# A delta-rule recurrence and a gated MLP on one core: weight pieces 768 columns wide, a shared gate and value bank, and a new division of PSUM

## The chip, the core and the metric

The kernel runs on one core of one Trainium2 chip. Its engines are TensorE (PE in the profile, its weight loads PEld), VectorE (DVE), ScalarE (ACT), GpSimd (POOL) and SyncE (SP, whose queue issues most of the transfers). The metric is the device time of one execution in microseconds (us), the median of several runs. The result must agree with a float32 reference.

## The reference

Four batches of eight heads run a delta rule over 768 tokens with head size 48; the 32 sequences are then read as 3072 tokens of 384 features for a gated MLP.

```python
k_n = k / (np.linalg.norm(k, axis=-1, keepdims=True) + 1e-06)
for t in range(S):
    kt, vt, bt = (k_n[:, :, t], v[:, :, t], beta[:, :, t, None])
    y[:, :, t] = np.einsum('bhd,bhde->bhe', q[:, :, t], state)
    v_old = np.einsum('bhde,bhd->bhe', state, kt)
    state = state + bt[:, :, :, None] * np.einsum('bhd,bhe->bhde', kt, vt - v_old)
...
gate = 1.0 / (1.0 + np.exp(-(x @ w_gate)))
val = x @ w_val
return (gate * val @ w_out).astype(np.float32)
```

The three weight matrices (384 x 1536 twice, 1536 x 384) arrive as float64 and are turned into float32 on the chip.

## The kernel before

**Recurrence.** The 768 tokens are cut into 12 groups of 64 (`g` = 0 to 11). Inside a group the recurrence is a triangular system: `gram` makes the products of all keys of a group, ScalarE and VectorE copy them to a tile G (`block`) with tokens along the free axis, `norms` takes the keys' norms from its diagonal and makes `gam` (beta over the squared norm) and `mq` (the norm, by which V is multiplied in `scale_v`), and a solve on VectorE inverts the system with two instructions a step. Groups are solved in pairs. For groups 0 and 1, `solve_pair` takes halves of 16 tokens (15 steps), transposes the result into `mt` (L334), and TensorE joins the halves: `pz`, a copy of it on ScalarE, `pm`, and a subtraction on VectorE (`closing`, L343), with a transpose (`flipped`, L339) ahead of `pm`. Later pairs are solved in 31 steps (`solve`, L298 and L301) and transposed at L303. After that come, for each group, the products with the state (`pk`), their subtraction from V (`less`, L384), the new rows (`updates`, `pu`, in steps 0 to 2), the output rows (`rows`, `yy`, from keys and queries masked on VectorE, L271) and the state's advance (`pd`). `flip` transposes the output rows into the MLP's input, split into two fp32r parts, high and low.

**Weights.** A weight piece is 128 x 384. There are 36, each loaded by one transfer of 384 KB (`load_piece`), and five instructions make it ready: on ScalarE `tail_bits` (L150), `rescale` (L155) and `weight_hi` (L167), on VectorE `join` (L162) and `weight_lo` (L172).

**MLP.** A tile is one unit of tokens by one of the 12 slices of the hidden layer. Groups 0 and 1 are a unit of 256 columns each (`single` tiles, 24 in all); later pairs of groups share a unit of 512 columns (`wide` tiles, 60). Each tile has nine matmuls for the gate and nine for the value (`gate_val`, L503), a sigmoid on ScalarE (L508), a product on VectorE (L513), a split into two parts (L518 on ScalarE, L523 on VectorE) and nine matmuls into three output banks (`outp`, L538). At a unit's end ScalarE copies the banks into `ot` tiles (L550) and SP stores them (L556).

**PSUM and SBUF.** The eight PSUM banks are three for the recurrence (`ps_aux`), two for gates and values, three for outputs (which some steps of groups 0 and 1 borrow). The tiles `u` (a joined weight piece) and `ot` share one SBUF tag of three buffers.

**Order.** No loop sets the order. Every step above is a `task` with an engine, an estimated cost, the tasks it follows, and the banks or buffers it takes and frees; `schedule` simulates the engines with those estimates, picks on each engine the ready task with the highest urgency (path length, the table URGENCY, a lift for the recurrence's words), and the kernel is then written out in that order. So each engine runs a fixed sequence, and what the estimates miss shows as waiting. Where the simulated TensorE has nothing to do ahead of the first gate, dummy matmuls on zeros (`warm_up`) are written in. Transfers are held back: at most EARLY groups of them are in flight up to the task named in QUIET (`pm0`), FLIGHT behind it, and the weight pieces from number HUSH on wait for that task.

Of the kernel before, what the change touches and what calls it, by code (L numbers as in the profile page):

```python
# [58 lines left out]
def deltanet_gated_mlp(ctx: ExitStack, tc: tile.TileContext, kd, qd, kv, beta, words, out):  # L59
# [97 lines left out]
    us = {}  # L157

    def join(n):
        half, lo, hi = words_of(n)  # L160
# [1 line left out]
        nc.vector.scalar_tensor_tensor(out=u, in0=hi, scalar=3, in1=lo, op0=ALU.logical_shift_left, op1=ALU.bitwise_or)  # L162

    def weight_hi(n):
        f, w = pieces[n]
        parts[w, f] = t = wt.tile([128, 2, PW], F32R, name=f"w_{n}", tag=f"w{n}")
        nc.scalar.copy(t[:, 0], us[n].bitcast(F32))  # L167
# [57 lines left out]
    def scale_v(g):  # L225
        V, mq = state[g]["v"], state[g - g % 2]["mq"]
        if g < 2:
            nc.vector.tensor_tensor(out=V, in0=V, in1=mq[:, :, g:g + 1].to_broadcast([128, CP, D]), op=ALU.mult)
# [751 lines left out]
```

## Time and profile before

| | |
|---|---|
| median of 3 runs | 657.55 us (654.12 to 658.02) |
| the profiled execution | 657.68 us |
| its span from the first to the last instruction | 656.0 us |
| PE busy | 624.8 us, 95% |
| PEld busy (beside PE) | 505.6 us, 77% |
| DVE busy | 389.0 us, 59% |
| ACT busy | 299.1 us, 46% |
| POOL busy | 10.1 us, 2% |
| moved by DMA | 40.77 MB |

The rows quoted further down are of the profiled execution. A row of a group names the line, the engine, the operation, output <- input and the shapes; behind the bar stand busy time, mean ns of one, and the idle time of the engine just ahead of such instructions with what ended it. A row of a timeline gives the start in us, the length, the engine and the instruction, and in square brackets how long the engine had stood still and what ended that. Busy shares are means over the whole span: the span has a first stretch in which TensorE has little work, and then one of tiles, and their limits differ.

### The profile page before, as it was taken

What the parts mean: (1) busy time and instruction counts of PE and PEld (TensorE: products, weight loads), DVE (VectorE), ACT (ScalarE), POOL (GpSimd) and SP (SyncE); (2) the same over time, 40 slices, a digit from 0 to 9 for tenths busy, and PEclk for the clock granted to TensorE, in tenths of its full rate; (3) what the DMA queues carried; (4) which work ended last, traced back from release to release, by engine and by line L of the source; (5) the groups of instructions that cost most, each with busy time, mean ns of one, the idle gap of its engine ahead of it and who ended that gap; (6) DMA issues with size and microseconds to landing.
All of it is one profiled execution on the core that took longest, in us unless ns stands there. A gap on an engine that the chain in (4) does not pass through costs nothing.

```text
span 656.0 us, 21070 instructions
## 1 busy us (share of the span) xinstructions
PE 624.8 (95%) x9420; PEld 505.6 (77%) x9420; DVE 389.0 (59%) x891; ACT 299.1 (46%) x720; POOL 10.1 (2%) x25
## 2 busy tenths in 40 slices
PE   8977898988999999999999999999999999999997
PEld 4446788977988787887778777778887778888886
DVE  4987859984589752599543499633699433221221
ACT  5777896445441635434415532724535323221212
POOL 3000000000000000000000000000000000000000
PEclk9978989999899999999999999999999999999999
DMA  8866650013130030120131021041020000010001
GB/s 274 266 165 203 195 171 26 1 27 107 29 82 24 26 84 27 33 74 25 27 108 34 2 72 48 4 108 35 1 73 25 3 2 3 0 49 0 1 0 49
DMA packets 16075, 40.77 MB, mean 62 GB/s; under 512 B 2929, under 2 KB 3697, under 8 KB 15985
## 3 DMA queue, kind: packets, MB, share of 16 engines
q1 hardware_dynamic: 15984, 39.43, 20.3%
q8 instruction: 74, 1.21, 0.8%
q14 instruction: 17, 0.13, 0.1%
HBM read 34.70 MB, written 4.72 MB: 60 GB/s over the span
## 4 chain that ended last, share of the span: by engine, by line
PE 66%; DVE 16%; DMA 9%; ACT 5%; issue 3%; SPq 1%; DVEq 0%
PE gv_g L503 18%; PE gv_v L503 18%; PE po L538 18%; DMA raw<-in_words_dram 6%; DVE tmp L298 3%; DVE X L301 3%; PE pu L405 3%; PE yy L433 2%; PE yy L436 1%; DVE sg L513 1%; ACT G L251 1%; PE pp L266 1%; DVE h L523 1%; PE pt L485 1%; PE pk L375 1%
## 5 line engine op out<-in xcount | busy, mean ns | idle before, releaser
L538 PE MATMUL po<-h,w 128*128 128x512 f32 (+1 forms) x756 | 169.9, 368 | 3.2 <-DVE h L523 2.6
L503 PE MATMUL gv_v<-xx,w 128*128 128x512 f32 (+1 forms) x756 | 167.4, 365 | 2.9 <-DVE w L172 2.4
L503 PE MATMUL gv_g<-xx,w 128*128 128x512 f32 (+1 forms) x756 | 168.0, 367 | 0.1
L538 PEld LDWEIGHTS po<-h,w 128*128 128x128 f32 x756 | 128.2, 189 | 28.3 <-DVE h L523 3.5
L503 PEld LDWEIGHTS gv_v<-xx,w 128*128 128x128 f32 x756 | 127.7, 189 | 26.6 <-DVE w L172 2.6
L503 PEld LDWEIGHTS gv_g<-xx,w 128*128 128x128 f32 x756 | 127.3, 189 | 23.3 <-DVE w L172 0.3
L513 DVE TENSOR_TENSOR sg<-sg,gv_v 128x512 f32<-128x512 f32 (+1 forms) x84 | 51.2, 609 | 124.1 <-PE gv_v L503 112.7
L518 ACT CAST h<-sg 128x512 fp32r<-128x512 f32 (+1 forms) x84 | 46.9, 559 | 150.6 <-DVE sg L513 150.3
L508 ACT ACTIVATE sg<-gv_g 128x512 f32<-128x512 f32 (+1 forms) x84 | 45.0, 536 | 97.8 <-PE gv_g L503 97.1
L523 DVE TENSOR_TENSOR h<-sg,h 128x512 fp32r<-128x512 f32 (+1 forms) x84 | 51.4, 612 | 30.0 <-ACT h L518 29.5
L413 ACT COPY su<-pu 32x384 f32<-32x384 f32 x92 | 43.3, 470 | 45.6 <-PE pu L405 44.1
L298 DVE TENSOR_TENSOR tmp<-X,gp 128x31 f32<-128x31 f32 (+15 forms) x155 | 53.0, 342 | 4.4
L301 DVE TENSOR_TENSOR X<-X,tmp 128x31 f32<-128x31 f32 (+15 forms) x155 | 52.9, 341 | 3.8
L232 ACT ACTIVATE v<-v,mq 128x48 f32<-128x48 f32 x160 | 37.7, 322 | 8.9 <-DVE mq L222 8.9
L384 DVE TENSOR_TENSOR R<-v,pk 128x384 f32<-128x384 f32 x44 | 22.3, 548 | 24.9 <-PE pk L398 17.1
L271 DVE TENSOR_TENSOR kqp<-pp,pmask 64x512 f32<-64x512 f32 x48 | 32.4, 686 | 6.5 <-PE pp L266 5.9
L469 DVE TENSOR_TENSOR su<-su,pd 48x384 f32<-48x384 f32 x40 | 22.0, 551 | 17.0 <-PE pd L460 16.4
L251 ACT COPY G<-pg 32x256 f32<-32x256 f32 (+1 forms) x66 | 25.8, 392 | 12.2 <-PE pg L247 10.9
L181 PE MATMUL warm<-zero 128*128 128x512 bf16 x104 | 27.7, 418 | 1.0 <-POOL half L116 1.0
L494 DVE TENSOR_TENSOR xx<-pt,xx 128x384 fp32r<-128x384 f32 x24 | 12.8, 554 | 21.7 <-ACT xx L492 21.4
L405 PEld LDWEIGHTS pu<-R,mt 32*32 32x32 f32 x1408 | 16.9, 105 | 11.2 <-issue 7.7
L405 PE MATMUL pu<-R,mt 32*32 32x48 f32 x1408 | 20.1, 203 | 4.7 <-issue 2.5
(89 smaller groups left out, 459.3 us busy)
## 6 DMA issues: line engine op xcount, KB each, us to landing
raw<-in_words_dram SPq DMA_DIRECT2D x36, 384.0 KB, 4.0
kqp<-in_qd_dram SPq DMA_DIRECT2D x24, 256.0 KB, 3.9
kqp<-in_kd_dram SPq DMA_DIRECT2D x24, 192.0 KB, 3.5
v<-in_kv_dram SPq DMA_DIRECT2D x12, 384.0 KB, 4.0
k<-in_kv_dram SPq DMA_DIRECT2D x12, 384.0 KB, 3.2
out_dram<-ot SPq DMA_DIRECT2D x15, 256.0 KB, 2.0
out_dram<-ot SPq DMA_DIRECT2D x6, 128.0 KB, 2.7
beta<-in_beta_dram SPq DMA_DIRECT2D x6, 16.0 KB, 4.0
```

The source lines that it names most:

```text
L232: nc.scalar.activation(V[:, c], V[:, c], AF.Copy, scale=mq[:, c, g % 2:g % 2 + 1])
L271: nc.vector.tensor_tensor(out=kq[t:t + 64, sec], in0=pp[e][t:t + 64], in1=pmask[t:t + 64, e].unsqueeze(1).to_broadcast([64, J, C]), op=ALU ...
L298: nc.vector.tensor_tensor(out=tmp, in0=X[:, j:32, j:j + 1].to_broadcast([128, n, j]), in1=gp[:, j:j + 1, 0:j].to_broadcast([128, n, j]), o ...
L301: nc.vector.tensor_tensor(out=X[:, j:32, 0:j], in0=X[:, j:32, 0:j], in1=tmp, op=ALU.add)
L405: nc.tensor.matmul(out=pu[0 if g else x][r:r + 32, j], lhsT=mt[r:r + 32, g % 2, e * J + j], rhs=R[e][r:r + 32, j], start=True, stop=True)
L413: nc.scalar.copy(su[r:r + 32, 3 if x else e], pu[0][r:r + 32])
L503: nc.tensor.matmul(out=pg, lhsT=parts[w, f][:, a, k * 128:(k + 1) * 128], rhs=x[b][:, k], start=(k == 0 and q == 0), stop=(k == KC - 1 and ...
L508: nc.scalar.activation(h, st["g", f], AF.Sigmoid)
L513: nc.vector.tensor_tensor(out=h, in0=h, in1=st["v", f], op=ALU.mult)
L518: nc.scalar.copy(hh[:, 0], st["sg", f])
L523: nc.vector.tensor_tensor(out=hh[:, 1], in0=st["sg", f], in1=hh[:, 0].bitcast(F32), op=ALU.subtract)
L538: nc.tensor.matmul(out=po[k], lhsT=parts["o", f][:, w, k * 128:(k + 1) * 128], rhs=hh[:, a], start=begins(p, f) and q == 0, stop=ends(p, f ...
```

## The change

- **Weight pieces.** 18 pieces of 768 columns: gate and value of one slice of the hidden layer ("gv"), or the output weights of two slices ("oo"). Each comes in two transfers of 384 KB and is converted by the same five instructions, each over 768 columns. EARLY is 3 and HUSH 6 (pieces, so twelve transfers).
- **PSUM.** Four banks for the recurrence, two for gates and values, two for outputs. A single tile's gate and value share a bank, and so do two of its three output parts; the third output bank of a wide tile comes from `ps_aux`. The masked products of group 0 move to `ps_out`, its `pk` and `pu` to `ps_aux`.
- **`u` and `ot`** have two buffers instead of three.
- **Norms.** `gam` is made from s² + 2 EPS s + EPS² right behind the root; the steps for the norm m come after it, and the solve now waits for `gam` alone. One step more.
- **`scale_v`** is one VectorE instruction for every group; for groups 2 to 11 it was 16 small ones on ScalarE.
- **Transfers.** One of group 0's two key transfers is issued by ScalarE.
- **`rows`** leaves out the products with the state for group 0, which are zero.
- **Order.** A single tile's gate and value are one task; estimates, URGENCY and the lifts have new numbers.

```diff
-EARLY, FLIGHT, HUSH = 4, 2, 15
+EARLY, FLIGHT, HUSH = 3, 2, 6
...
-    ps_aux = ctx.enter_context(tc.tile_pool(name="ps_aux", bufs=3, space=PSUM))
+    ps_aux = ctx.enter_context(tc.tile_pool(name="ps_aux", bufs=4, space=PSUM))
...
-    ps_out = ctx.enter_context(tc.tile_pool(name="ps_out", bufs=3, space=PSUM))
+    ps_out = ctx.enter_context(tc.tile_pool(name="ps_out", bufs=2, space=PSUM))
...
+        if g == 0:
+            nc.scalar.dma_start(*pairs.pop())
+        move(pairs)
...
+    pieces = []
+    for f in range(0, NF, 2):
+        pieces += [(f, "gv"), (f + 1, "gv"), (f, "oo")]
...
+    def load_piece(n, part):
+        if part == 0:
+            raw[n] = wt.tile([128, 2 * PW, 2], U32, name=f"raw_{n}", tag=f"w{n}")
+        mine = slice(part * 2 * PW, (part + 1) * 2 * PW)
+        move([(raw[n].rearrange("p c w -> p (c w)")[:, mine], words[n, :, mine])])
...
-        us[n] = u = wk.tile([128, PW], U32, name=f"u_{n}", tag="u", bufs=3)
+        us[n] = u = wk.tile([128, 2 * PW], U32, name=f"u_{n}", tag="u", bufs=2)
...
+        nc.vector.scalar_tensor_tensor(out=m, in0=s, scalar=2 * EPS, in1=ss, op0=ALU.mult, op1=ALU.add)
+        yield
+        nc.vector.tensor_scalar(out=m, in0=m, scalar1=EPS * EPS, scalar2=None, op0=ALU.add)
+        yield
+        st["gam"] = gam = wk.tile([128, 32], F32, name=f"gam_{g}", tag="gam", bufs=2)
+        nc.vector.reciprocal(gam, m)
...
-        nc.vector.tensor_tensor(out=t, in0=m, in1=m, op=ALU.mult)
-        yield
-        st["gam"] = gam = wk.tile([128, 32], F32, name=f"gam_{g}", tag="gam", bufs=2)
-        nc.vector.reciprocal(gam, t)
...
-        if g < 2:
-            nc.vector.tensor_tensor(out=V, in0=V, in1=mq[:, :, g:g + 1].to_broadcast([128, CP, D]), op=ALU.mult)
-            yield
-            return
-        for c in range(CP):
-            nc.scalar.activation(V[:, c], V[:, c], AF.Copy, scale=mq[:, c, g % 2:g % 2 + 1])
-            yield
+        nc.vector.tensor_tensor(out=V, in0=V, in1=mq[:, :, g % 2:g % 2 + 1].to_broadcast([128, CP, D]), op=ALU.mult)
+        yield
...
-            for part in range(2):
+            for part in range(0 if g else 1, 2):
...
+        if w == "g" or p > 1:
+            whole = ps_gv.tile([128, 512], F32, name=f"gv_{p}_{f}_{w}", tag="gv")
+            st["g", f], st["v", f] = (whole[:, 0:GT], whole[:, GT:2 * GT]) if p < 2 else (whole if w == "g" else st["g", f], whole)
+        pg = st[w, f]
...
-        st["ot", k] = ot = wk.tile([128, st["width"]], F32, name=f"ot_{p}_{k}", tag="u", bufs=3)
+        st["ot", k] = ot = wk.tile([128, st["width"]], F32, name=f"ot_{p}_{k}", tag="u", bufs=2)
...
-    URGENCY = {"G2": 16500, "L2": -3500, "T0": 10500, "bits/15": 26000, "bits/18": 7000, "gate0": 500, "gate1": -500, "gram0": -10500, "hh0": -15500, "hl0": 11000,
...
+    URGENCY = {"D0": -6500, "G3": -1000, "bits/0": -2000, "bits/12": -8500, "bits/15": 18500, "dk2": -3000, "dv1": -4500, "gate1": 1000, "gram3": 1500, "hh1": 500,
...
-    HEAD, LIFT, CHAIN = 60000, 20000, set("gram pk pp u yy pd pt less s y xh xl T D z pz pm m sv G L".split())
+    LIFTS = {0: 60000, 1: 10000, 2: 0, 3: 0}
+    FIRST = set("gram u yy pt less y xh xl T D z pz pm sv G n h mt ll".split())
+    CHAIN = set("gram pk pp u yy pd pt less s y xh xl T D z pz pm m sv G L".split())
```

What follows shows three places on VectorE in the written order, before and after. A row is a line of the kernel, an operation, output<-input with the tiles' numbered names, and the shape; x2 is two alike in a row.

VectorE before, from the second Newton step of group 0's norms (`ny`, `nt`, `ns`, `m`) to the start of its solve (`stage` holds the solution, `gp` the products of keys). L271 is a mask.

```order
L202 SCALAR_TENSOR_TENSOR ny_0_269<-nt_0_270,ny_0_269 128x32
L204 TENSOR_TENSOR ns_0_271<-ny_0_269,gp_0_227 128x32
L206 SCALAR_TENSOR_TENSOR nt_0_270<-ns_0_271 128x32
L271 TENSOR_TENSOR kqp0_73<-pp_0_1_233,pmask_77 64x512
L208 TENSOR_TENSOR nt_0_270<-nt_0_270,gp_0_227 128x32
L210 SCALAR_TENSOR_TENSOR nt_0_270<-nt_0_270,ny_0_269 128x32
L212 SCALAR_TENSOR_TENSOR m_0_272<-nt_0_270,ns_0_271 128x32
L214 TENSOR_TENSOR nt_0_270<-m_0_272 128x32
L217 RECIPROCAL gam_0_367<-nt_0_270 128x32
L219 TENSOR_TENSOR gam_0_367<-gam_0_367,beta_0_119 128x32
L320 COPY stage_82<-gam_0_367 128x32
L323 SCALAR_TENSOR_TENSOR gp_0_227<-gp_0_227,gam_0_367 128x16x16 x2
```

After, the same place:

```order
L206 SCALAR_TENSOR_TENSOR ny_0_264<-nt_0_265,ny_0_264 128x32
L208 TENSOR_TENSOR ns_0_266<-ny_0_264,gp_0_250 128x32
L210 SCALAR_TENSOR_TENSOR m_0_267<-ns_0_266,gp_0_250 128x32
L212 TENSOR_SCALAR m_0_267<-m_0_267 128x32
L215 RECIPROCAL gam_0_327<-m_0_267 128x32
L217 TENSOR_TENSOR gam_0_327<-gam_0_327,beta_0_115 128x32
L219 SCALAR_TENSOR_TENSOR nt_0_265<-ns_0_266 128x32
L221 TENSOR_TENSOR nt_0_265<-nt_0_265,gp_0_250 128x32
L223 SCALAR_TENSOR_TENSOR nt_0_265<-nt_0_265,ny_0_264 128x32
L225 SCALAR_TENSOR_TENSOR m_0_267<-nt_0_265,ns_0_266 128x32
L321 COPY stage_82<-gam_0_327 128x32
L324 SCALAR_TENSOR_TENSOR gp_0_250<-gp_0_250,gam_0_327 128x16x16 x2
```

No mask stands among the norms any more, and `gam` is made ahead of the steps for m; those still stand ahead of the solve.

VectorE before, from the solve's transpose (into `mt`) to the subtraction that closes the join; `u` is a joined weight piece, `w` its fp32r parts, `v` a group's V, `pz` TensorE's product.

```order
L334 STREAM_TRANSPOSE mt_75<-stage_82 128x32x16x2
L339 STREAM_TRANSPOSE stage_82<-mt_75 128x512
L222 STREAM_TRANSPOSE mq_0_569<-m_0_272 128x32
L228 TENSOR_TENSOR v_0_118<-v_0_118,mq_0_569 128x768
L228 TENSOR_TENSOR v_1_124<-v_1_124,mq_0_569 128x768
L162 SCALAR_TENSOR_TENSOR u_0_643<-raw_0_206 128x384
L162 SCALAR_TENSOR_TENSOR u_2_646<-raw_2_219 128x384
L162 SCALAR_TENSOR_TENSOR u_1_650<-raw_1_230 128x384
L172 TENSOR_TENSOR w_0_648<-u_0_643,w_0_648 128x384
L162 SCALAR_TENSOR_TENSOR u_10_658<-raw_10_276 128x384
L172 TENSOR_TENSOR w_2_652<-u_2_646,w_2_652 128x384
L343 TENSOR_TENSOR mt_75<-mt_75,pz_0_501 128x512
```

After, the same place:

```order
L335 STREAM_TRANSPOSE mt_75<-stage_82 128x32x16x2
L233 TENSOR_TENSOR v_0_114<-v_0_114,mq_0_435 128x768
L340 STREAM_TRANSPOSE stage_82<-mt_75 128x512
L272 TENSOR_TENSOR kqp0_73<-pp_0_0_287,pmask_77 64x512 x2
L272 TENSOR_TENSOR kqp0_73<-pp_0_1_288,pmask_77 64x512 x2
L233 TENSOR_TENSOR v_1_274<-v_1_274,mq_0_435 128x768
L165 SCALAR_TENSOR_TENSOR u_0_604<-raw_0_203 128x768
L165 SCALAR_TENSOR_TENSOR u_1_607<-raw_1_256 128x768
L344 TENSOR_TENSOR mt_75<-mt_75,pz_0_460 128x512
```

The four masks now stand here, the transpose for `mq` has gone ahead into the solve, and four joins and two low parts of 384 columns have become two joins of 768.

VectorE before, from the last steps of the solve of groups 2 and 3 (`tmp`, `X`) over its transpose to the subtractions for group 2 (`R`); `sg` and `h` belong to single tiles, named by unit and slice (`h_1_9`).

```order
L298 TENSOR_TENSOR tmp_2_2_2426<-X_2_1825,gp_2_1802 128x60
L513 TENSOR_TENSOR sg_1_9_2390<-sg_1_9_2390,gv_1_9_v_2397 128x256
L301 TENSOR_TENSOR X_2_1825<-X_2_1825,tmp_2_2_2426 128x30x2
L298 TENSOR_TENSOR tmp_2_1_2442<-X_2_1825,gp_2_1802 128x31
L301 TENSOR_TENSOR X_2_1825<-X_2_1825,tmp_2_1_2442 128x31
L303 STREAM_TRANSPOSE mt_75<-X_2_1825 128x32x16x2
L523 TENSOR_TENSOR h_1_9_2440<-sg_1_9_2390,h_1_9_2440 128x256
L172 TENSOR_TENSOR w_30_1864<-u_30_1772,w_30_1864 128x384
L384 TENSOR_TENSOR R_2_0_2450<-v_2_1144,pk_2_0_2355 128x384
L384 TENSOR_TENSOR R_2_1_2462<-v_2_1144,pk_2_1_2356 128x384
```

After, the same place:

```order
L299 TENSOR_TENSOR tmp_2_2_2167<-X_2_1676,gp_2_1636 128x60
L225 SCALAR_TENSOR_TENSOR m_2_1674<-nt_2_1672,ns_2_1673 128x32
L302 TENSOR_TENSOR X_2_1676<-X_2_1676,tmp_2_2_2167 128x30x2
L228 STREAM_TRANSPOSE mq_2_2171<-m_2_1674 128x32
L299 TENSOR_TENSOR tmp_2_1_2173<-X_2_1676,gp_2_1636 128x31
L233 TENSOR_TENSOR v_2_938<-v_2_938,mq_2_2171 128x768
L302 TENSOR_TENSOR X_2_1676<-X_2_1676,tmp_2_1_2173 128x31
L517 TENSOR_TENSOR sg_1_7_2078<-sg_1_7_2078,gv_1_7_g_2038 128x256
L304 STREAM_TRANSPOSE mt_75<-X_2_1676 128x32x16x2
L385 TENSOR_TENSOR R_2_0_2192<-v_2_938,pk_2_0_2129 128x384
L385 TENSOR_TENSOR R_2_1_2213<-v_2_938,pk_2_1_2130 128x384
L527 TENSOR_TENSOR h_1_7_2190<-sg_1_7_2078,h_1_7_2190 128x256
```

The norm steps for m, the transpose for `mq` and V's scaling now stand between the solve's last steps, the transpose comes two tiles sooner in the row of tiles, and the subtractions follow it directly.

More of the change, by code (lines that the diff above doesn't have):

```diff
@@ L96, in load_k @@
     def load_k(g):
-        move([(kqp[g % 2][64 * e:64 * e + D, 0:2].rearrange("p s c t -> p (s c t)"), kd[g, e]) for e in range(2)])
+        pairs = [(kqp[g % 2][64 * e:64 * e + D, 0:2].rearrange("p s c t -> p (s c t)"), kd[g, e]) for e in range(2)]
+        if g == 0:
+            nc.scalar.dma_start(*pairs.pop())
+        move(pairs)
     def load_q(g):
@@ L370, in rest @@
         kq = kqp[g % 2]
-        st["pk"] = pk = [(ps_aux if g else ps_out).tile([128, J, D], F32, name=f"pk_{g}_{e}", tag="aux" if g else "po") for e in range(2)]
+        st["pk"] = pk = [ps_aux.tile([128, J, D], F32, name=f"pk_{g}_{e}", tag="aux") for e in range(2)]
         for j in range(J):
@@ L400, in updates @@
             return
-        st["pu"] = pu = [(ps_out if x else ps_aux).tile([128, J, D], F32, name=f"pu_{g}_{step}_{x}", tag="po" if x else "aux") for x in range(1 if g else 2)]
+        st["pu"] = pu = [ps_aux.tile([128, J, D], F32, name=f"pu_{g}_{step}_{x}", tag="aux") for x in range(1 if g else 2)]
         for j in range(J):
@@ L533, in outp @@
         if begins(p, f):
-            st["po"] = [ps_out.tile([128, st["width"]], F32, name=f"po_{p}_{f}_{k}", tag="po") for k in range(KC)]
+            banks = [(ps_aux if n > 1 else ps_out).tile([128, 512], F32, name=f"po_{p}_{f}_{n}", tag="aux" if n > 1 else "po") for n in range(3 if p > 1 else 2)]
+            st["po"] = banks if p > 1 else [banks[k // 2][:, k % 2 * GT:(k % 2 + 1) * GT] for k in range(KC)]
         hh, po = st["hh", f], st["po"]
@@ L629, in lengths @@
             got += new
-        n = steps(f"n{g}", DVE, norms(g), [1240] + [195] * 14 + [350, 195, 205], got, take=("gp", "mq"))
-        by_name[n[16]]["after"].append(by_name[f"dv{g}"])
+        n = steps(f"n{g}", DVE, norms(g), [1240] + [195] * 11 + [350, 195] + [195] * 4 + [205], got, take=("gp", "mq"))
+        by_name[n[GAMMA]]["after"].append(by_name[f"dv{g}"])
         if g:
@@ L649, in pair @@
             costs += [157 + 1.04 * (32 - j) * j] * 2
-        h = steps(f"h{g}", DVE, gen, costs, [n[-2], f"X{g}"])
+        h = steps(f"h{g}", DVE, gen, costs, [n[GAMMA + 2], f"X{g}"])
         by_name[h[-1]]["free"] = ("gp",)
@@ L663, in halves @@
             costs += [157 + 1.04 * 2 * (16 - j) * j] * 2
-        h = steps("h0", DVE, gen, costs, [n[-2]])
+        h = steps("h0", DVE, gen, costs, [n[GAMMA + 2]])
         by_name[h[-1]]["free"] = ("gp",)
@@ L682, in recurrence @@
             joins(1)
+        bank = "aux" if g else "po"
         sv = scale_v(g)
-        by = [f"dv{g}", f"n{g - g % 2}.17"]
-        for i in range(1 if g < 2 else 4):
-            by = [task(f"sv{g}.{i}", *((DVE, 950) if g < 2 else (ACT, 1020)), lambda: [next(sv, None) for _ in range(4)], by)]
+        by = [f"dv{g}", f"n{g - g % 2}.18"]
+        by = [task(f"sv{g}.0", DVE, 950, lambda: next(sv, None), by)]
         scaled = by[0]
@@ L751, in out_of @@
         wide = len(UNITS[p]) > 1
-        task(f"out{i}", PE, 2080 if wide else 1080, lambda: outp(p, f), [f"hl{i}", f"wlo{number[f, 'o']}"] + has(f"out{i - 1}") + (cleared if begins(p, f) else []), take=("po",) * 3 if begins(p, f) else (), free=("h",))
+        task(f"out{i}", PE, 2080 if wide else 1080, lambda: outp(p, f), [f"hl{i}", f"wlo{number[f // 2 * 2, 'oo']}"] + has(f"out{i - 1}") + (cleared if begins(p, f) else []), take=("po", "po") + ("aux",) * wide if begins(p, f) else (), free=("h",))
         if ends(p, f):
```

97 lines of the change are left out of this document (49 added, 48 removed), and 10 rows, old and new, of the table URGENCY.

## The prediction

> **What bounds the kernel now.** I read the busy time by stage first, then TensorE's rows in order of time, then VectorE's. Columns of the first view: stretch, its length, busy time of PE, PEld, DVE, ACT, POOL, granted TensorE clock, DMA share, GB/s.
>
> ```profile
> span 656.0 us, 21070 instructions
> ...
> 0.00:58.71 58.71, 47.39 (x1231) 27.93 (x1231) 44.24 (x108) 39.92 (x86) 5.18 (x20) 0.91 0.76 231
> ...
> 190.50:300.00 109.50, 108.43 (x1369) 87.48 (x1361) 74.52 (x180) 44.94 (x108) 1.00 (x1) 1.00 0.16 46
> ...
> L181 PE MATMUL warm<-zero 128*128 128x512 bf16 x104 | 27.7, 418 | 1.0 <-POOL half L116 1.0
> ```
>
> From 190.5 us on PE is busy 99%, at full clock, on matmuls that the change leaves alone. The time to be won lies before. Up to the first gate matmul at 58.71 PE is busy 47.4 us, of which 27.7 are dummy `warm` matmuls: 58.7 - (47.4 - 27.7) = 39.0 us without real work. So I follow one number, the lead: how much sooner the changed kernel has done the same work.
>
> ```profile
> 6.63 2.09 PE L247 MATMUL pg<-kqp 48*64 48x64 f32 x126 [0.60 <-DMA kqp<-in_kd_dram]
> ...
> 33.90 1.26 PE L357 MATMUL pz<-stage 32*32 32x32 f32 x125 [1.76 <-issue]
> 35.09 1.03 PE L181 MATMUL warm<-zero 128*128 128x512 bf16 x2
> 36.19 0.28 PE L405 MATMUL pu<-v,mt 32*32 32x48 f32 x1
> 37.74 1.50 PE L405 MATMUL pu<-v,mt 32*32 32x48 f32 x63 [1.26 <-issue]
> ...
> 58.71 1.32 PE L503 MATMUL gv_g<-xx,w 128*128 128x256 f32 x9
> ...
> 11.93 0.19 DVE L193 TENSOR_SCALAR n<-gp 128x32 int32<-128x32 int32 x1
> ...
> 12.59 0.69 DVE L271 TENSOR_TENSOR kqp<-pp,pmask 64x512 f32<-64x512 f32 x1
> ...
> 18.28 0.20 DVE L320 COPY stage<-gam 128x32 f32<-128x32 f32 x1
> ...
> 27.84 1.95 DVE L334 STREAM_TRANSPOSE mt<-stage 128x1024 f32<-128x1024 f32 x1
> ...
> 30.66 1.83 DVE L228 TENSOR_TENSOR v<-v,mq 128x768 f32<-128x768 f32 x2
> ...
> 35.45 0.69 DVE L343 TENSOR_TENSOR mt<-mt,pz 128x512 f32<-128x512 f32 x1
> ```
>
> The chain to the first gate is VectorE's: norms, solve, transpose, then the join that ends at L343 and frees the first `pu` matmuls. Two "issue" waits stand in it. Between them lie 125 + 2 + 1 = 128 matmuls with a weight load each, so 256 PE instructions: PE runs out of instructions at even distances in its program, and the wait returns wherever 256 of them pass faster than the next batch arrives.
>
> **The change, step by step.** *Norms and masks of group 0.* From 11.93 to 18.28 VectorE takes 6.35 us, with four masks of 0.69 among the norm steps (2.74). The masks move behind the solve, one norm step is added and one moves into the solve; 19 steps at the 0.22 us spacing of such rows are 4.1, so 2.3 us are won. One key transfer goes to ScalarE's queue, ahead of its table load, where nothing waits before gram 0; that then starts without the 0.60 wait and the half-row before it, about 0.9. One `mq` transpose inside the solve costs 0.2. Lead at the transpose L334: 3.0.
>
> *What VectorE does next.* Between that transpose and the join L343 it now has, in order: one V scaling, a 512-wide transpose, four masks, the other V scaling, two 768-wide weight joins: 0.92 + 0.67 + 2.74 + 0.92 + 1.83 = 7.1 us (1.83 for two being the 128x768 row). From 26.8 that ends at 33.9, against 35.45: the lead shrinks to 1.5. It hides the fetch wait, though: while VectorE is busy the batch for `pu` arrives, so most of the 1.26 goes. Lead after `pu`: 2.3. Through the two further update steps, keeps, `pz`, flips (same lengths as before, with one more fetch wait covered) it comes to about 4.3: first gate near 54.4. By then `pk` of group 1 is done (1.1) and `pm` not yet (1.5): even.
>
> *Wide weight pieces.* 36 pieces become 18, with the same bytes.
>
> ```profile
> L150 ACT ACTIVATE raw<-raw 128x384 int32<-128x384 uint16 x36 | 19.3, 551 | 9.8 <-DMA raw<-in_words_dram 9.8
> ...
> L167 ACT CAST w<-u 128x384 fp32r<-128x384 f32 x36 | 17.7, 510 | 5.1 <-DVE u L162 4.9
> ...
> L172 DVE TENSOR_TENSOR w<-u,w 128x384 fp32r<-128x384 f32 x36 | 19.9, 554 | 7.9 <-ACT w L167 7.8
> ...
> L518 ACT CAST h<-sg 128x512 fp32r<-128x512 f32 x60 | 37.2, 620 | 132.9 <-DVE sg L513 132.7
> ...
> L518 ACT CAST h<-sg 128x256 fp32r<-128x256 f32 x24 | 9.7, 405 | 17.8 <-DVE sg L513 17.6
> ...
> 60.00:97.00 37.00, 32.96 (x711) 30.46 (x710) 25.23 (x52) 32.98 (x81) 0.00 (x0) 0.95 0.68 198
> ...
> 58.71:96.10 37.39, 4.85 (x9) 0.95 0.67 197
> ...
> 58.71:96.10 37.39, 5.68 (x11) 0.95 0.67 197
> ...
> 58.71:96.10 37.39, 7.38 (x15) 0.95 0.67 197
> ```
>
> A ScalarE row grows (620 - 405)/256 = 0.84 ns per column; 384 more make 0.87, 0.87 and 0.83 us for two of 0.55 (L150), 0.55 (L155, same shape) and 0.51 (L167). A piece saves 0.64 us there; VectorE, by the 0.92 row, about 0.19 on each of two. From 60 to 97 ScalarE is busy 33 of 37 us, so this is the stretch where it pays. The last three rows are L150, L155 and L167 alone between the first gate and the last copy of G for groups 2 and 3: 35 narrow rows, 17.9 us. In the new order 16 wide ones stand there, 13.7 by the durations above. That copy comes up to 4.2 sooner still. Bounds for the lead there: 4.3 (nothing gained) and 8.5; I take 7.5, nearer the upper end since ScalarE is 89% busy.
>
> *Transfers.* SP issues as many weight transfers as before, each as large. Twelve instead of fifteen go out before the pause at `pm`, so 1.2 MB more follow it, 5.9 us at 199 GB/s (row below), less the 2 us by which it starts sooner and the 384 KB of group 1's k now put behind them. Hidden: the fifth and later gates, two tiles of 3.2 us and the recurrence of group 1 behind the first, wait for them; if not, 4 us at most. The third output bank of wide tiles comes from the pool of the recurrence, which keeps the three it had: nothing.
>
> *The solve of groups 2 and 3.*
>
> ```profile
> 96.13 1.25 DVE L189 STREAM_TRANSPOSE gp<-G 128x1024 f32<-128x1024 f32 x1 [0.30 <-ACT G L251]
> ...
> 102.52 0.19 DVE L289 COPY X<-gam 128x32 f32<-128x32 f32 x1
> ...
> 136.00 1.90 DVE L303 STREAM_TRANSPOSE mt<-X 128x1024 f32<-128x1024 f32 x1
> ...
> 139.68 0.88 PE L405 MATMUL pu<-R,mt 32*32 32x48 f32 x64
> ...
> PE gv_v L503 <- DVE w L172: 2.4, 1, 2.4
> ...
> 102.52:136.00 33.48, 33.26 (x384) 32.45 (x382) 31.60 (x94) 15.10 (x54) 0.00 (x0) 1.00 0.05 13
> 136.00:190.53 54.53, 47.69 (x1244) 43.70 (x1242) 32.67 (x72) 27.77 (x67) 0.99 (x1) 0.97 0.21 55
> ```
>
> X starts with a lead of 8.0 (two norm steps fewer before it). From X to the transpose VectorE is busy 31.6 of 33.5 us. Taken out: four product or split steps (18 become 14, 0.42 each) and four masks: 4.4. Put in: one wide join, its low part, V's scaling, two norm steps: 3.2. So 32.3 us; transpose near 126.8, lead 9.2. But PE was full there (33.26 of 33.48), and the order now lets only tiles through whose products stand ahead of the transpose: PE waits for VectorE, some 5 to 8 us in small pieces, and arrives at `pu` of group 2 one tile (2.15 + 1.07) short. Behind the transpose (1.9) stand two subtractions (1.0), a split (0.4), an `out` (1.1) and `pu` (0.9): it ends near 132.2 instead of 140.6, and 8.4 - 3.2 = 5.2.
>
> *To the wide tiles.* After that PE has work. Before, it idled 6.8 us from 136 to 190.5, of which 2.4 (on L172) ahead of `pu`, and ran a group at low clock after a fetch wait (below, 0.8): 5.2 us. I leave 4 of such waits in the new order and win 1.2, with bounds of 5.2 and, should they double, -5: lead 6.4.
>
> *V on VectorE* costs 0.95 a group on an engine 68% busy from 190.5 to 300 (74.5 of 109.5), and frees ScalarE: nothing, as long as products stay ahead of PE; bounds 0 and the ten scalings, 9.5.
>
> *One bank for gate and value.* The sigmoid now starts after the value half.
>
> ```profile
> 102.53 1.24 PE L503 MATMUL gv_g<-xx,w 128*128 128x256 f32 x9
> ...
> 103.86 0.38 ACT L508 ACTIVATE sg<-gv_g 128x256 f32<-128x256 f32 x1 [0.52 <-PE gv_g L503]
> ```
>
> Now it is released by the gate half, at 103.86, while the value half still runs: 1.07 us later in future, on 24 tiles. The product comes no sooner than the value half anyway, two tiles have banks, and `out` stands two gates behind: hidden; if not, up to 24 x 1.07 = 26. The Trainium skill ("PSUM — Partial Sum Buffer", on bank collisions) has two engines on one bank and quadrant raise an error, so that wait cannot be tuned away; no run here shows a collision. By that rule the sum is the same, with the 26 as its far end.
>
> *Tail.* `ot` has two buffers instead of three.
>
> ```profile
> 651.08 1.98 ACT L550 COPY ot<-po 128x512 f32<-128x512 f32 x3 [1.39 <-PE po L538]
> 651.69 1.73 SPq L556 DMA_DIRECT2D out_dram<-ot  x3
> ```
>
> The third copy, at 652.46, now waits until the first store, issued at 651.69, has landed, 2 us or more later; copy and store follow. Loss 0.5 to 1.7; I take 1.1.
>
> Sum: 6.4 - 1.1 = 5.3 us; span 650.7. The profiled execution took 657.68 for a span of 656.0, 0.13 above the median of 657.55: 650.7 + 1.7 = **652.4 us**.
>
> **Rivals.** *Faster: PE never starves in the solve.* If VectorE, which stands still 1.9 us there, fits the products in sooner, the lead of 9.2 survives: 656.0 - 9.2 - 1.2 + 1.1 + 1.7 = 648.4. Against it: the order is fixed.
>
> *The lead does not arise.* ScalarE's copy of `pz` stands behind the conversion of the fifth wide piece, whose second half is the tenth weight transfer.
>
> ```profile
> 20.00:25.00 5.00, 5.00 (x24) 2.27 (x23) 4.45 (x17) 3.95 (x9) 0.00 (x0) 1.00 0.96 327
> ...
> 40.00:60.00 20.00, 15.34 (x572) 11.47 (x571) 16.39 (x33) 14.11 (x32) 0.00 (x0) 0.87 0.68 199
> ```
>
> With four transfers in flight 327 GB/s, with two 199; now three. Up to that half 6.4 MB must land between about 3 and 27.3 us: 263 GB/s decides, which is just the middle. At 199 it lands at 35, the join slips to 37.7, 2.2 later than before, and the later savings only pay that back: 656 to 658.
>
> *Slower: the clock.*
>
> ```profile
> 164.09 0.46 PE L405 MATMUL pu<-R,mt 32*32 32x48 f32 x24 [2.30 <-issue]
> 164.48 2.06 PE L503 MATMUL gv_g<-xx,w 128*128 128x256 f32 x9
> ```
>
> After a gap of 2.3 us a group of nine took 2.06 instead of 1.24. If PE's waits in the solve come in gaps that long, its tiles there cost 3 x 0.82 = 2.5 more each; over seven tiles 17, of which the 5 to 8 us of waiting absorb a part: 10 net, 662. It decides at gaps of about 2 us; mine are 1 to 1.3. The Trainium skill ("TensorE: Matmul & The Clock Gate", "What's actually happening") has the clock halve after an idle window of about 3.4 us. By that rule this rival is dead; the row above shows a slow group after only 2.3, so it keeps a chance.
>
> **How the numbers follow.** Forecast 0.50 (its own range 649 to 656), faster rival 0.20, no lead 0.23, slower 0.07. About 1% (6.6 us) is what a measurement of this kernel can tell from no change. Under 651.0: the faster rival and nearly half of the forecast, 0.43; slower by over 1%: 0.06; the rest, 0.51. The range runs from 645.5, the faster rival with some 3 us of play for waits that go as well, to 657.5, the case without a lead.
>
> **What would show it.** Right: L334's row near 24.9; first gate near 54.4; G's last copy for groups 2 and 3 near 88.6; its solve's transpose near 126.8, with PE idle before it on VectorE's products; first 512-wide gate near 184; the last `ot` copy waiting on a DMA. Wrong: ScalarE's copy of `pz` late on a weight transfer; new long waits of PE after 190; a granted clock under 0.9 between 95 and 130.

## The result and the profile after

| | before | after |
|---|---|---|
| median of 4 runs | 657.36 us (654.12 to 658.02) | 641.15 us (639.20 to 641.97) |
| ratio, 95% interval | | 0.976 (0.972 to 0.980) |
| profiled execution, its span | 657.68, 656.0 | 641.97, 640.2 |

The change gained 16.2 us; 5.3 were forecast, and the range ended at 645.5. The sign was right, the size was not. Three executions further down were far off (995, 2054 and 3350 us), and the medians leave them out.

The page of the changed kernel, with the busy times by engine and the row of the dummies:

```profile
span 640.2 us, 20758 instructions
...
PE 622.9 (97%) x9391; PEld 505.1 (79%) x9391; DVE 393.4 (61%) x871; ACT 256.2 (40%) x506; POOL 10.1 (2%) x25
...
L185 PE MATMUL warm<-zero 128*128 128x512 bf16 x107 | 30.1, 438 | 1.0 <-POOL half L119 1.0
```

PE's idle time fell from 31.2 (656.0 - 624.8) to 17.3 us, and the dummies grew by 2.4: 11.5 of the 15.8 us by which the span is shorter. The rest is busy time: by form, the matmuls of 256 columns (single tiles) take 88.9 us instead of 94.8, some others a little more, and group 0 leaves out 32 matmuls. It is not the clock: the mean granted clock of the two executions is 0.987 before and 0.985 after.

Busy time by stretch (stretch, its length, PE, PEld, DVE, ACT, POOL, clock, DMA share, GB/s), before:

```profile
58.71:96.13 37.42, 33.38 (x719) 30.88 (x712) 25.65 (x54) 32.60 (x79) 0.00 (x0) 0.95 0.67 197
...
140.56:190.53 49.97, 45.52 (x1171) 42.00 (x1170) 28.11 (x65) 26.88 (x65) 0.99 (x1) 0.97 0.22 60
190.53:648.08 457.55, 455.00 (x5762) 364.15 (x5757) 247.54 (x546) 175.03 (x416) 2.95 (x3) 1.00 0.11 33
```

and after:

```profile
56.12:86.74 30.62, 30.55 (x784) 29.02 (x778) 24.66 (x38) 29.79 (x57) 0.00 (x0) 1.00 0.70 208
...
131.20:176.53 45.33, 45.33 (x1145) 43.22 (x1143) 28.78 (x61) 28.23 (x67) 0.96 (x1) 1.00 0.22 62
176.53:630.92 454.39, 453.72 (x5816) 363.28 (x5811) 256.60 (x564) 145.47 (x287) 2.99 (x3) 1.00 0.12 34
```

The three pairs are: first gate to the transposition of G for groups 2 and 3, the end of group 2's first `pu` to the first wide gate, and the wide tiles up to the last outputs. In each PE stood still before (4.0, 4.5 and 2.6 us, length less PE) and hardly does so after (0.1, 0 and 0.7).

VectorE's timeline after, with the marks that the prediction followed (start, length, instruction):

```profile
24.94 1.97 DVE L335 STREAM_TRANSPOSE mt<-stage 128x1024 f32<-128x1024 f32 x1
...
34.27 0.69 DVE L344 TENSOR_TENSOR mt<-mt,pz 128x512 f32<-128x512 f32 x1 [0.49 <-issue]
...
86.74 1.25 DVE L193 STREAM_TRANSPOSE gp<-G 128x1024 f32<-128x1024 f32 x1 [1.42 <-ACT G L252]
...
92.82 0.19 DVE L290 COPY X<-gam 128x32 f32<-128x32 f32 x1
...
124.81 2.00 DVE L304 STREAM_TRANSPOSE mt<-X 128x1024 f32<-128x1024 f32 x1
```

and TensorE's:

```profile
32.89 1.29 PE L358 MATMUL pz<-stage 32*32 32x32 f32 x115 [2.22 <-issue]
...
36.71 1.33 PE L406 MATMUL pu<-v,mt 32*32 32x48 f32 x54 [1.12 <-issue]
...
56.12 2.36 PE L507 MATMUL gv_g<-xx,w 128*128 128x256 f32 x18
...
118.12 3.44 PE L507 MATMUL gv_g<-xx,w 128*128 128x256 f32 x18 [2.85 <-DVE sg L517]
...
130.33 0.88 PE L406 MATMUL pu<-R,mt 32*32 32x48 f32 x64 [0.86 <-DVE kqp L272]
...
176.53 2.35 PE L507 MATMUL gv_g<-xx,w 128*128 128x512 f32 x9
...
630.92 4.36 PE L543 MATMUL po<-h,w 128*128 128x512 f32 x18
```

Gain by stage (us; measured: the before mark less the after mark, and differences of these):

| stage | forecast | measured |
|---|---|---|
| to the first gate | 4.3 | 2.6 |
| to the transposition of G | 3.2 | 6.8 |
| to the end of `pu` 2.0, less the tile (3.2) that PE is behind | -2.3 | -3.3 |
| to the first wide gate | 1.2 | 7.9 |
| wide tiles | 0 | 3.2 |
| tail | -1.1 | -1.4 |
| sum | 5.3 | 15.8 |

### The profile page after: what moved, and what is told of

Its sections match the earlier page's. It is cut to its first block, busy times and chain, and to the rows that moved or that the text cites. A ratio compares the mean times of both kernels' runs of the same rounds, so it can differ in the third digit from the quotient of the medians.

```text
span 640.2 us, 20758 instructions
## 1 busy us (share of the span) xinstructions
PE 622.9 (97%) x9391; PEld 505.1 (79%) x9391; DVE 393.4 (61%) x871; ACT 256.2 (40%) x506; POOL 10.1 (2%) x25
## 4 chain that ended last, share of the span: by engine, by line
PE 84%; DVE 7%; ACT 5%; issue 2%; DMA 2%; SPq 0%; ACTq 0%
PE gv_g L507 23%; PE po L543 21%; PE gv_v L507 19%; PE warm L185 4%; PE pu L406 3%; PE pk L376 2%; PE yy L437 2%; PE yy L434 2%; PE pp L267 2%; DVE X L302 1%; PE pt L486 1%; PE pk L399 1%; PE pg L248 1%; PE pd L461 1%; DVE tmp L299 1%
## 5 line engine op out<-in xcount | busy, mean ns | idle before, releaser
L507 PE MATMUL gv_g<-xx,w 128*128 128x512 f32 (+1 forms) x972 | 194.2, 349 | 3.9 <-DVE sg L517 3.3
L507 PEld LDWEIGHTS gv_g<-xx,w 128*128 128x128 f32 x972 | 152.9, 190 | 28.2 <-DVE sg L517 3.9
L507 PE MATMUL gv_v<-xx,w 128*128 128x512 f32 x540 | 135.6, 395 | 0.0
L507 PEld LDWEIGHTS gv_v<-xx,w 128*128 128x128 f32 x540 | 100.2, 188 | 22.5
L517 DVE TENSOR_TENSOR sg<-sg,gv_v 128x512 f32<-128x512 f32 x60 | 41.2, 686 | 95.6 <-PE gv_v L507 94.1
L272 DVE TENSOR_TENSOR kqp<-pp,pmask 64x512 f32<-64x512 f32 x48 | 32.3, 686 | 6.8 <-PE pp L267 6.3
L185 PE MATMUL warm<-zero 128*128 128x512 bf16 x107 | 30.1, 438 | 1.0 <-POOL half L119 1.0
L185 PEld LDWEIGHTS <-zero 128*128 128x128 bf16 x107 | 11.0, 109 | 15.1 <-issue 5.2
```

The source lines that it names most:

```text
L185: nc.tensor.matmul(out=hot[0], lhsT=z.to_broadcast([128, 128]), rhs=z.to_broadcast([128, 512]), start=True, stop=True)
L272: nc.vector.tensor_tensor(out=kq[t:t + 64, sec], in0=pp[e][t:t + 64], in1=pmask[t:t + 64, e].unsqueeze(1).to_broadcast([64, J, C]), op=ALU ...
L507: nc.tensor.matmul(out=pg, lhsT=parts[w, f][:, a, k * 128:(k + 1) * 128], rhs=x[b][:, k], start=(k == 0 and q == 0), stop=(k == KC - 1 and ...
L517: nc.vector.tensor_tensor(out=h, in0=h, in1=st["v", f], op=ALU.mult)
```

## The experiments

Medians are of the run named; the changed kernel's is 641.15, and the kernel before, run beside each group, had medians of 655.6 to 657.4. "In place" means that the written order stays as it was.

**Width undone in place** (each of the five instructions likewise):

```diff
-        nc.scalar.copy(t[:, 0], us[n].bitcast(F32))
+        for c in (slice(0, PW), slice(PW, 2 * PW)):
+            nc.scalar.copy(t[:, 0, c], us[n][:, c].bitcast(F32))
```

> The changed kernel in the same order, but each of the five instructions of a weight piece is issued as two of 384 columns. Per piece this puts 0.6 us on ScalarE and 0.4 us on VectorE. Theory (the width pays because ScalarE is full from the first gate to the last copy of G, 29.8 of 30.6 us): 20 wide rows stand there, 0.19 us each, so that copy ends some 3.8 us later than 86.7, the transpose at L304 near 128.5, and the time is 643.5 to 646. Rival (the gain is in the order and the waits, and the width is hidden): the copy moves by less than 1.5 us and the time stays within 640 to 642.5.

643.78 us (641.34 to 645.59), 2.6 slower, though the runs overlap with those of the changed kernel (639.20 to 641.97). In the profiles the span is 1.6 longer (641.8). VectorE's timeline in this run:

```profile
88.42 1.25 DVE L198 STREAM_TRANSPOSE gp<-G 128x1024 f32<-128x1024 f32 x1 [1.77 <-ACT G L257]
...
126.64 2.02 DVE L309 STREAM_TRANSPOSE mt<-X 128x1024 f32<-128x1024 f32 x1
```

G is transposed 1.7 later and the solve 1.8, and that stays to the end. The width pays on this path, but with half of the 3.8 that counting ScalarE's rows gave.

**V back on ScalarE in place:**

```diff
+        if g < 2:
             nc.vector.tensor_tensor(out=V, in0=V, in1=mq[:, :, g % 2:g % 2 + 1].to_broadcast([128, CP, D]), op=ALU.mult)
+        else:
+            for c in range(CP):
+                nc.scalar.activation(V[:, c], V[:, c], AF.Copy, scale=mq[:, c, g % 2:g % 2 + 1])
```

> The changed kernel in the same order, but V of groups 2 to 11 is scaled by 16 ScalarE instructions a group at the place of the one on VectorE (about 3.8 us a group on ScalarE, 0.95 less on VectorE). Theory (as in the prediction: where V is scaled costs nothing as long as nothing stands behind it): 640 to 643. Rival (the scaling stands right ahead of the subtractions and of ScalarE's own splits, so its 3.8 us are waited for): the wait of 0.9 at the first pu of group 2 becomes about 3, and other groups add up to 1 us each: 645 to 652.

646.96 us (645.49 to 648.21), 5.8 slower. ScalarE's timeline for group 3, TensorE's wait behind it, and the waits of VectorE in the wide tiles (line waited for, total, times, longest):

```profile
138.57 3.71 ACT L237 ACTIVATE v<-v,mq 128x48 f32<-128x48 f32 x16
142.29 1.92 ACT L418 COPY su<-pu 32x384 f32<-32x384 f32 x4
```
```profile
144.26 1.14 PE L438 MATMUL yy<-su,kqp 48*64 48x48 f32 x62 [1.47 <-ACT su L418]
```
```profile
DVE R L389 <- ACT v L237: 9.7, 6, 2.0
```

The scaling holds up the copies of `pu` (ScalarE) and the subtractions (VectorE). The wide tiles take 457.05 (177.92 to 634.97): of the 3.2 us that the change won there, 2.7 are lost again. As much is lost ahead of them: from the solve's transposition (123.55) to the first wide gate it takes 54.4 instead of 51.7. The rival was right: here V on VectorE is worth 5.8 us.

**The same alone in the kernel before**, first at the place of the first of the 16, then where the changed kernel has it. In the second run, some groups subtracted from V before it was scaled; the third mends that.

```diff
         for c in range(CP):
-            nc.scalar.activation(V[:, c], V[:, c], AF.Copy, scale=mq[:, c, g % 2:g % 2 + 1])
+            if c == 0:
+                nc.vector.tensor_tensor(out=V, in0=V, in1=mq[:, :, g % 2:g % 2 + 1].to_broadcast([128, CP, D]), op=ALU.mult)
             yield
```

> The kernel before in its own order, with only one thing changed: V of groups 2 to 11 is scaled by one VectorE instruction a group at the place of the first of the 16 on ScalarE. Theory (putting V back on ScalarE cost the changed kernel 5.8 us, half of it ahead of the first wide tile and half behind it, because 3.8 us of scaling stood in ScalarE's row ahead of copies that TensorE waits for): about the same is won here, 650.5 to 654. Rival (the gain needs the new order, in which ScalarE has nothing else ahead of those copies): under 1.5 us, 656 to 658.

> The kernel before in its own order with V scaled on VectorE, as in the run where that made it slower, but at the places where the changed kernel has it: for an even group right ahead of the solve's transposition, for an odd one right ahead of its first subtraction. Theory (what counts is where the scaling stands: in the middle of the solve it pushes back the subtractions and splits of tiles, at these places it takes ScalarE's 3.8 us away and costs VectorE 0.95 at an idle moment): 650 to 655. Rival (VectorE's 0.95 in the chain of the solve costs as much as ScalarE's relief brings, wherever it stands): 656 to 663.

> As the run with V late in the kernel before, but each group's V is now scaled on VectorE ahead of whatever uses it first (the solve's transposition or the group's first subtraction); there, some groups subtracted from V before it was scaled. Theory (place decides): 650 to 655. Rival (0.95 us a group in VectorE's chain costs what ScalarE's relief brings): 656 to 663.

662.75, 662.73 and 660.92 us: ratios 1.010 (1.005 to 1.016), 1.008 (1.005 to 1.011) and 1.006 (1.003 to 1.008) to the kernel before. All three are slower. TensorE in the wide tiles of the first:

```profile
228.81 0.27 PE L406 MATMUL pu<-R,mt 32*32 32x48 f32 x2 [2.00 <-DVE R L385]
...
422.92 0.88 PE L406 MATMUL pu<-R,mt 32*32 32x48 f32 x64 [1.33 <-DVE mt L304]
```

In the old order VectorE's chain is already what `pu` waits for (0.5 and 1.2 us at two such places), and 0.95 us a group makes it later. The theory of place fell: at none of the three places does V on VectorE gain in the old order, and in the new one it does.

**Three output tiles** (the third in a buffer that is free by then):

```diff
-tag="u", bufs=2)
+**(dict(tag="part", bufs=1) if p > 1 and k > 1 else dict(tag="u", bufs=2)))
```

> The changed kernel, but the third output tile of a wide unit lies in a buffer of its own, so the last copy does not wait for the first store. Theory (the tail lost 1.36 us: 9.28 from the start of the last output matmuls to the end, against 7.92 before): 1.0 to 1.4 us faster, 639.8 to 640.2 with the end near 638.9 in the profile. Rival (the store's landing sets the end anyway): no change.

639.82 us (638.50 to 640.29), 1.3 faster. ScalarE's last row in the changed kernel shows what went:

```profile
636.62 0.59 ACT L555 COPY ot<-po 128x512 f32<-128x512 f32 x1 [1.41 <-DMA out_dram<-ot]
```

**Instruction batches moved.** The first run puts tiny dummies at the end, the others split dummies of 512 columns into two of 256 (changed kernel with three output tiles, and the kernel before):

```diff
+        parts = 2 if len(hot) <= 32 else 1
+        hot.append(None)
+        for _ in range(parts):
-        nc.tensor.matmul(out=hot[0], lhsT=z.to_broadcast([128, 128]), rhs=z.to_broadcast([128, 512]), start=True, stop=True)
+            nc.tensor.matmul(out=hot[0][:, 0:512 // parts], lhsT=z.to_broadcast([128, 128]), rhs=z.to_broadcast([128, 512 // parts]), start=True, stop=True)
```

> The changed kernel with the last five dummy matmuls before the first gate replaced by fourteen tiny ones each: 130 PE instructions more (half of 256) in about the same time, so every later fetch of instructions falls half a batch elsewhere. Theory A (no fetch wait is left behind the first gate because a whole tile of 36 long instructions now stands between the short steps of the recurrence, wherever the batches end): no issue wait behind the first gate, 640 to 642. Theory B (the batches happen to end at good places): at least one issue wait of 1 to 2.3 us with a slow group of matmuls behind it, 643 to 647.

> The changed kernel with the third output buffer, and the first 32 dummy matmuls issued as two of 256 columns each: 64 PE instructions more (a quarter of a batch) in the same time, so the fetches behind them fall elsewhere at no cost of their own. Theory A (the new order leaves room for every fetch behind the first gate, wherever it falls): no issue wait over 0.5 us behind the first gate, and the time differs from 639.8 only by what the waits ahead of the first gate change: 638 to 642. Theory B (its batches end at good places): an issue wait of 1 us or more behind the first gate, with slow matmuls behind it, 642 to 645.

> The same with the first 64 dummies split: 128 PE instructions more, half a batch. Theory A: no issue wait over 0.5 us behind the first gate, 638 to 642. Theory B: one of 1 us or more, 642 to 645.

> The changed kernel with the third output buffer and the first 48 dummies split: 96 PE instructions more, between the best placement so far (64 more: 637.3) and the worst (128 more: 644.0). If the ends of the batches set the time, it lies between or beside them, 636 to 644, and the issue waits listed account for the difference to 637.3 within 2 us.

The first run took 646.24 us and tells the theories apart no further. TensorE's timeline in it:

```profile
51.58 1.64 PE L190 MATMUL warm<-zero 32*32 32x32 f32 x46
53.74 3.48 PE L190 MATMUL warm<-zero 32*32 32x32 f32 x94 [0.52 <-issue]
```

The 70 tiny dummies are 140 matmuls here. They took 5.1 us, and with 270 instructions more (280 less the 10 they replace) the ends moved by about a whole batch, which is hardly at all. With split dummies:

| PE instructions more | changed, three output tiles | before |
|---|---|---|
| 0 | 639.82 | 657.36 |
| 64 | 637.34 | 657.03 |
| 96 | 642.41 | |
| 128 | 644.03 | 658.14 |

TensorE's timeline at 128 more:

```profile
70.65 0.37 PE L409 MATMUL pu<-R,mt 32*32 32x48 f32 x15 [1.75 <-issue]
72.37 3.57 PE L510 MATMUL gv_g<-xx,w 128*128 128x256 f32 x18
```

A fetch wait inside the recurrence of group 1, with a slow tile behind it (3.57 against 2.36). Theory A fell: the order does not make room for every fetch. The placement moves the changed kernel by 6.7 us. The waits account for it in part: over the whole span the "issue" waits add up to 4.3 us at 64 more, 11.2 at 96 and 8.6 at 128, while the spans are 635.8, 641.8 and 643.1. At 96 that is within the 2 us expected, at 128 it is not. With 64 more the first gate comes at 52.83, with none at 56.49.

That these waits come from the ends of batches can be counted: in the kernel before, those up to 66 us stand behind 477, 605, 735, 991, 1118, 1246 and 1373 recorded matmuls, that is 128 or 256 from one another but for two records at most, and each matmul has its weight load, so 256 PE instructions or twice that.

> The kernel before with its last three dummy matmuls replaced by 22 tiny ones each, so that the fetches of instructions behind them fall half a batch elsewhere; the dummies themselves cost 2 to 4 us. Theory (before's wait of 2.3 at the pu of group 3 sits there because pk, one output and pu follow one another in 3 us, so some fetch wait comes back near it wherever the batches end): an issue wait of over 1 us between 140 and 195. Rival (it was where a batch happened to end): no issue wait of over 0.5 us behind the first gate, and the stretch from the solve's transposition to the first wide gate shorter by 3 to 4 us.

> The kernel before, with its first 32 dummy matmuls issued as two of 256 columns each: 64 PE instructions more in the same time, so its fetches fall a quarter of a batch elsewhere. In the changed kernel that was worth 2.5 us, and half a batch cost 4.2. Theory (a large part of the gain of 16.2 was the kernel before having its batches end at bad places, above all the wait of 2.3 and the slow groups at 164): that wait is gone or under 0.5, and the time is 650 to 654. Rival (where one wait goes another comes, so the kernel before stands at about its mean): 655 to 659.

> The same with the first 64 split, half a batch. Theory: the stretch from the transposition of groups 2 and 3 to the first wide gate is 50 to 52 us as in the run with tiny dummies, against 54.5, and the time 650 to 654. Rival: 655 to 659.

659.02, 657.03 and 658.14 us: not faster (ratios to the kernel before, run beside them, 1.0035, 1.0025 and 1.0039). The tiny dummies of the first moved the ends by a whole batch again. In all three the wait at 164 us is gone; with 128 more, the stretch from the solve's transposition to the first wide gate is 50.5 us instead of 54.5 (VectorE, TensorE, and TensorE ahead of its first gate):

```profile
139.40 1.91 DVE L306 STREAM_TRANSPOSE mt<-X 128x1024 f32<-128x1024 f32 x1
```
```profile
189.89 2.37 PE L506 MATMUL gv_g<-xx,w 128*128 128x512 f32 x9
```
```profile
62.32 1.35 PE L463 MATMUL pd<-su,k 64*48 64x48 f32 x50 [2.86 <-issue]
```

The last row is a wait that came in its place. But the wait at 164 also comes and goes with the ends where they were. In the run with V on VectorE at the first place, whose TensorE row is that of the kernel before, it is this:

```profile
168.22 0.46 PE L406 MATMUL pu<-R,mt 32*32 32x48 f32 x24 [1.39 <-issue]
```

and in the two runs with V late it is not there at all: 2.30, 1.39, 0, 0 at one place. These kernels differ in where V is scaled, so the times of the other engines differ as well. So the ends of the batches alone do not fix it, and it is not the gain either: over the placements 0, 64 and 128 the means are 640.4 and 657.5 us, 17.1 apart, 15.8 without the third output tile's 1.3.

**Numbers of the order.** The table URGENCY emptied (`URGENCY = {}`) in both kernels:

> The changed kernel with the table URGENCY empty, so the planner orders by path lengths and lifts alone. Theory S (pieces, banks and V carry the gain): this kernel is about as much faster than the kernel before with an empty table as the two are apart now, 12 to 20 us. Theory N (the new numbers carry a large part): the two come within 6 us of each other. Either way both are slower than with their numbers: 645 to 660 here.

> The kernel before with the table URGENCY empty, beside the run above. Theory S: 660 to 675, 12 to 20 us above the changed kernel without its table. Theory N: within 6 us of it.

647.86 us (646.23 to 650.48) and 657.05 (656.14 to 661.08): 9.2 apart. The new numbers are worth 6.7 us to the changed kernel; the old ones to the kernel before nothing that can be measured (1.002, 0.999 to 1.005). It fell between the two theories. The 9.2 still hold the new estimates and lifts, which these two runs leave as they were.

**Parts undone with a new plan.** Gate and value as two tasks; the norms in the old order; three banks for the recurrence. In the first two each split on ScalarE also follows that of the tile before:

```diff
-            task(f"gate{i}", PE, 2160, lambda: (gate_val(p, f, "g"), gate_val(p, f, "v")), ready, take=("gv",), free=over)
+            task(f"gate{i}", PE, 1080, lambda: gate_val(p, f, "g"), ready, take=("gv",))
+            task(f"val{i}", PE, 1080, lambda: gate_val(p, f, "v"), [f"gate{i}"], free=over)
...
-    copies, GAMMA = {}, 13
+    copies, GAMMA = {}, 14
...
-    ps_aux = ctx.enter_context(tc.tile_pool(name="ps_aux", bufs=4, space=PSUM))
+    ps_aux = ctx.enter_context(tc.tile_pool(name="ps_aux", bufs=3, space=PSUM))
```

> The changed kernel with gate and value of a single tile as two tasks again, in one bank as before and with the sigmoid behind both; the order is planned anew, so that other matmuls may stand between the halves. Theory (a row of 18 matmuls takes 2.27 us between short ones where two rows of nine took 1.32 and 1.21, so each tile that is torn apart costs 0.25 us): 1 to 3 us slower, 642 to 644.5. Rival (short steps that come sooner are worth the turn): 639 to 641.5.

> The changed kernel with the norms in the old order (the factor for the solve made last, from m squared), planned anew. Theory (three steps of 0.22 us fewer ahead of each solve: the first chain is 0.7 shorter, and in the wide tiles TensorE no longer waits the 1.5 + 0.7 us on mt and R that it waited before): 1.5 to 3 us slower, with waits of pu on mt or R behind 190 us. Rival (VectorE has that much time to spare there): within 1 us, and no such waits.

> The changed kernel with three banks for the recurrence instead of four (one of the eight stays unused; group 0's masked products and pk go back to where the kernel before had them), planned anew. Theory (the fourth bank lets gram of group 3 start before the copies of group 2's products have freed theirs, which is why the last copy of G came 1.9 us sooner than predicted): that copy comes at 90 to 94 and the time is 644 to 650. Rival (as predicted, the recurrence needs only the three it had): the copy within 2 us of 86.7, and no more than 3 us slower, which is about what a new plan alone shifts.

648.00, 643.43 and 784.15 us. The first lost 6.9, but where tiles are torn apart nothing was lost: from the solve's transposition to the first wide gate it took 50.2 us against 51.7. It lost 4.3 up to G's transposition (91.06) and 2.5 in the wide tiles, which the edit doesn't touch. That is the new plan, so neither theory is shown. The second lost 2.3, none of it in the wide tiles (454.7 against 454.4); nor did the waits of `pu` on `mt` or R that I expected there come back. The third is no fair test: a wide tile takes one of the three banks, which leaves the recurrence two, one fewer than the kernel before had, and PE's clock falls to 0.87. Only its G, transposed at 97.22 while no wide tile runs yet, bears on the fourth bank: 10.5 later than with four, under another order.

## Why the prediction was wrong, and where it was right

*Norms and masks*: right. The transposition was put near 24.9 and stands at 24.94.

*What VectorE does next*: the join was put at 33.9 and stands at 34.27, but "most of the 1.26 goes" was wrong: 1.12 of it stayed, and `pz` waited 2.22 instead of 1.76, so the first gate came at 56.12 instead of 54.4.

*Wide pieces*: mechanism right, size off twice. The width gives 1.7 on the path, not 3.2 (the run with narrow rows). My count of rows was off as well: 20 wide rows fell in this stretch, 17.4 us, and not 16 with 13.7. The other 5 us of that stage were not in my sum. ScalarE's and TensorE's waits before, in that stretch:

```profile
ACT raw L155 <- DMA raw<-in_words_dram: 2.9, 2, 2.1
ACT raw L150 <- DMA raw<-in_words_dram: 2.2, 1, 2.2
```
```profile
82.66 1.84 PE L247 MATMUL pg<-kqp 48*64 48x64 f32 x62 [2.37 <-ACT ys L451]
```

The chain that ended last, before (start, length, what), at the same place:

```profile
80.34 3.45 DMA raw<-in_words_dram
83.82 1.90 ACT raw L155 x4
```

ScalarE's old order put conversions ahead of the copies of group 1, and they stood there until a transfer landed; TensorE then waited for the copies. Before, that chain runs along transfers from 35.7 to 83.8 us; after, none stands in it between 6.8 and 140 us. The new order has no such wait (ScalarE is busy 29.8 of 30.6 us). This is read from the rows; no run undoes it alone. I read ScalarE's 89% as "busy" and did not ask what the other 11% waited for.

*Transfers*: hidden in the changed kernel, as forecast.

*The solve of groups 2 and 3*: right up to the transposition, 32.0 us behind X (32.3 forecast), and at `pu` TensorE had done 16 tiles where before it had done 17. Up to the end of `pu` the stage still lost 1.0 more than forecast (3.3 against 2.3). The slow tile at 118.12 (3.44) is the clock rival, at one place instead of seven, and the rows behind it were slow as well:

```profile
122.25 1.95 PE L376 MATMUL pk<-su,kqp 48*64 48x48 f32 x62 [0.17 <-DVE su L470]
124.12 2.13 PE L543 MATMUL po<-h,w 128*128 128x256 f32 x9
```

Elsewhere such rows take 1.15 and 1.23. In slices of 1 us the granted clock is 0.50 from 120 to 125.

*To the wide tiles*: this is the step that failed most. "I leave 4 of such waits in the new order" - none was left, and the gain was 7.9, beyond the bound of 5.2. Of the 50 us before, 4.5 were idle. The bound counted one slow group, but a second one followed it at a low clock (0.50 from 165 to 168 us):

```profile
166.34 2.06 PE L538 MATMUL po<-h,w 128*128 128x256 f32 x9
```

The two cost 1.7 together; the remaining 1.7 of the stage I can't assign to rows. The wait of 2.3 with its slow groups was no fixed part of the work: in the three runs with the dummies of the kernel before changed it is gone, and the stretch is 3.4 to 4.0 us shorter. I carried it into the new order as if it belonged to the work. Counted by cause and not by rows, 1.9 of the 7.9 need V on VectorE, which my sum put at nothing: with V back on ScalarE the stage takes 47.2 instead of 45.3.

*V on VectorE*: "nothing" was wrong. ScalarE's 3.8 us stand ahead of copies and subtractions in this order and cost 5.8. My bound of nine and a half stood on VectorE's side only; the gain's side was never bounded, though ScalarE's row was in the profile. In the kernel before the same edit loses 4 to 6, so this price could not be read from either order alone.

*One bank for gate and value*: mostly hidden. In the single tiles, which alone share a bank, TensorE never waited for a sigmoid, but twice for a product, which frees the bank (3.3 us, of which 2.85 at 118.12). Whether the shared bank or VectorE's order made it wait, no run separates.

*Tail*: right, 1.36 lost (9.28 from the last outputs to the end, 7.92 before) against 1.1.

*The wide tiles*: the sum took them as untouched. PE's idle time there fell from 2.6 to 0.7, and the stretch by 3.2; with V on ScalarE 2.7 of it come back.

*The clock*: after waits of 2.85 and 1.75 us tiles took 3.44 and 3.57 instead of about 2.3. The Trainium skill ("TensorE: Matmul & The Clock Gate", "What's actually happening") has the clock halve after an idle window of about 3.4 us; these rows do not agree. Nor does the length of the wait alone decide, as I had it with "about 2 us": in the kernel before the granted clock fell to 0.50 after waits of 2.30 and 2.37 (164.09 and 82.66), but stayed at 1.00 after 2.39 and 2.62 (138.66 and 101.61).

What stays open: how the 9.2 us without numbers divide among the fourth bank, the joined gate and value, the norms, and the new estimates and lifts. The first three were each tried under a new plan only, and new numbers for the order alone move the time by 6.7 us.

The fastest version is the changed kernel with three output tiles and 32 dummies split: 637.34 us (636.64 to 637.53), ratio 0.969 (0.966 to 0.972) to the kernel before.

## What to carry to other kernels

In a kernel whose engines run fixed sequences, list every wait of the bounding engine and ask whether it belongs to the work or to the order: the second kind may vanish in a new order, and the range must reach to where all of them have gone. Bound an edit that moves work between engines on both engines, and in the new order, not in the old. To compare two such kernels, move the ends of the instruction batches in both (split dummies do it at no cost), since one placement can be worth as much as a part of the change.
